# Local attention and a squared-ReLU MLP in one kernel: how the probabilities of the last three blocks are transposed

## The chip, the cores and the metric

The kernel runs on one core of a Trainium2 chip. The metric is the device time of one execution in microseconds (us). The times of the kernel before are 823.29, 822.72 and 823.01 us, median 823.01. A core has a matrix engine (TensorE, "PE" in the profile, with its weight loads as "PEld"), VectorE (DVE), ScalarE (ACT), GpSimd (POOL) and SyncE (SP), which here only issues DMA transfers. SBUF is the on-chip memory of 128 partitions, PSUM the accumulation memory that TensorE writes.

## The reference

```python
def _attn_ref(q, k, v):                       # 8 batches, 8 heads, 576 tokens, 64 wide; chunks of 64 tokens
    scores = scale * np.matmul(q_c, k_c.transpose(0, 1, 2, 4, 3))
    scores = scores - np.max(scores, axis=-1, keepdims=True)
    attn = np.exp(scores)
    attn = attn / (np.sum(attn, axis=-1, keepdims=True) + 1e-09)
    out = np.matmul(attn, v_c)
...
def _moe_ref(x, w_in, w_out, s, b):           # 4608 tokens, 512 -> 2048 -> 512
    h = x @ w_in
    r = np.maximum(h, 0.0)
    g = s * (r * r) + b
    return (g @ w_out).astype(np.float32)
```

All in float32. The output of the attention, tokens by 512, is the input x of the MLP.

## The kernel before

The 4608 tokens are 36 tiles of 128. A first stage computes four of them and prepares the weights; then come four blocks of eight tiles (`Block`; block 1 is the subclass `Second`). Each block is a list of steps. A step is twelve matmuls of 128x128 by 128x512 on TensorE, three for each float32 product, since every operand is held as a high and a low part ("gh" and "gl" for the down layer, "xh" and "xl" for the up layer). Blocks 2, 3 and 4 have 28 up steps and 28 down steps, seven products of half-size blocks in place of eight, whose sums VectorE forms (class `Chain`); block 1 has 32 up steps in the ordinary way, beside which it combines the weights of the later blocks (`combine`), and 28 down steps. Work that goes beside the matmuls is hung on the step before which it is written: `pre[step]` is a list of calls that every engine gets in this order. So the program fixes the order on every engine; an engine runs ahead or behind as its semaphores allow.

Beside its own matmuls each block computes the attention of the next block's tokens, in four groups of two tiles. In blocks 2 and 3 the groups begin at steps 3, 14, 25 and 36, in block 1 at 5, 17, 30 and 42 (`GROUPS`); below, a group is called by its first step, so "group 25 of block 2". Counted from its first step n, a group does (`plan_attention`): loads of q, k and v at n-3; at n the scores, 32 matmuls of 64x64 into PSUM (S, line 207); at n+1 the row maxima and the subtraction on VectorE (lines 212, 216); at n+2 the exponential on ScalarE; at n+3 the row sums, at n+4 the division ("norm", lines 228 to 230), all on VectorE; at n+7 eight transposes of 128x128 on TensorE into PSUM (T, line 237); at n+8 two copies of these to SBUF on ScalarE (line 242); at n+9 the product with v, 32 matmuls of 64x64 (V, line 249); at n+10 two copies of the result on ScalarE (line 273). S, T and V all take their PSUM tile from the pool `ps_a`, which has one buffer: whichever comes next waits until the engine that reads the one before has done so.

The other PSUM tiles come from `ps`, three buffers. Nearly all SBUF tiles come from one pool of 45 buffers (`slots`). The weights of each step are streamed from DRAM by SP, 512 KB a step, requested six steps ahead into six buffers (line 372), so SP keeps pace with TensorE; SP works in order, and an instruction that waits holds all behind it. GpSimd does the remaining sums, 128x1024 in float32, in the down steps of blocks 2 to 4 (line 413), and the differences of x (line 353); in block 1 those of line 413 are on VectorE.

Of the kernel before, what the change touches and what calls it, by code (L numbers as in the profile page):

```python
# [27 lines left out]
def local_attention_then_squared_relu_mlp(ctx: ExitStack, tc, qkv, w, s, b, out):  # L28
    nc = tc.nc
    P = 128  # L30
    NTB, NPAIR = qkv.shape[0], w.shape[1]
    NJ = 2 * NPAIR
    DM = out.shape[0]
    HALF = DM // 2
    CH = D = 64
    H = DM // D
    NHP = H // 2
    LAG = 3
    N = 2
    G = N * NHP  # L40
    NPP = NPAIR // 2
    BLOCK = 8
    assert NTB % BLOCK == 4

    const = ctx.enter_context(tc.tile_pool(name="const", bufs=1))
# [10 lines left out]
    def slot(dtype=F32, name="s"):  # L56
        return slots.tile([P, 2, DM], dtype, name=name, tag="s")
# [29 lines left out]
    class Pair:  # L87


        def __init__(self, k):  # L90
            self.layer, self.k = sequence[k]
            self.words = self.f = None
# [86 lines left out]
    class Attention:  # L179
        def __init__(self, tb, bank, x=None, col=0):  # L180
            self.tb, self.bank = tb, bank
            self.x = x and [t[:, :, col:col + N * P].rearrange("p a (i t) -> p i a t", i=N) for t in x]

        def load_qk(self):
            t = [slot(name="qk") for _ in range(N)]
            for i in range(N):
                nc.sync.dma_start(out=t[i], in_=qkv[self.tb + i, :, 0:2, :])
            self.qk = [t.rearrange("p i (h t) -> p i h t", h=H) for t in t]

        def load_v(self):  # L190
            t = slot(name="v")
            for i in range(N):
                nc.sync.dma_start(out=t[:, i], in_=qkv[self.tb + i, :, 2, :])
            self.v = [t[:, i].rearrange("p (h d) -> p h d", h=H) for i in range(N)]
# [8 lines left out]
        def scores(self):  # L203
            self.ps = self.bank(0)[:, :, 0:G * CH].rearrange("p c (g k) -> p c g k", g=G)
            for i, hp, c, h, rows, cols in self.quarters():
                qk = self.qk[i]
                nc.tensor.matmul(out=self.ps[cols, c, i * NHP + hp, :], lhsT=qk[rows, 0, h, :], rhs=qk[rows, 1, h, :],  # L207
                                 start=True, stop=True)

# [29 lines left out]
        def copies(self):  # L239
# [2 lines left out]
                nc.scalar.copy(out=pT[:, i, :], in_=self.ps[:, i, :])  # L242
            self.pT = pT.rearrange("p i (a t) -> p i a t", a=NHP)

        def values(self, apart=False):
            tiles = [self.bank(2) for _ in range(N if apart else 1)]
            ps = [t[:, :, 0:G * CH].rearrange("p c (g t) -> p c g t", g=G) for t in tiles]
            for i, hp, c, h, rows, cols in self.quarters():
                nc.tensor.matmul(out=ps[i if apart else 0][cols, c, i * NHP + hp, :], lhsT=self.v[i][rows, h, :],  # L249
                                 rhs=self.pT[rows, i, hp, cols], start=True, stop=True)  # L250
            if apart:
                self.halves = [(ps[i][:, :, i * NHP:(i + 1) * NHP, :].rearrange("p c a t -> p a c t"),
                                *(x[:, i].rearrange("p a (c t) -> p a c t", c=2) for x in self.x)) for i in range(N)]
            elif self.x:
                self.halves = [(ps[0][:, c].rearrange("p (i a) t -> p i a t", i=N),
                                *(x[:, :, :, c * CH:(c + 1) * CH] for x in self.x)) for c in range(2)]
            else:
                self.xf = slot(name="xf").rearrange("p i (a t) -> p (i a) t", a=2)
                x = self.xf.rearrange("p a (i t) -> p i a t", i=N)
                self.halves = [(ps[0][:, c].rearrange("p (i a) t -> p i a t", i=N), x[:, :, :, c * CH:(c + 1) * CH])  # L260
                               for c in range(2)]
# [68 lines left out]
    class Block:  # L330
        UP, TILES, ORDER, GROUPS = 28, 56, (0, 2, 1, 3), (3, 14, 25, 36)

        def __init__(self, n):
            self.tb0 = 4 + (n - 1) * BLOCK
            self.groups = [Attention(self.tb0 + 2 * i, steady_bank) for i in self.ORDER]
# [150 lines left out]
            at(24, lambda: self.store(0, 1, self.down_chain.c12))  # L486
            at(28, lambda: self.store(1, 0, self.down_chain.c21))

        def plan_attention(self, n, a):
            self.at(max(n - 3, 0), a.load_qk, a.load_v)  # L490
            for k, *fs in ((0, a.scores), (1, a.peak, a.sub), (2, a.exp), (3, a.sum), (4, a.norm),
                           (7, a.transposes), (8, a.copies), (9, a.values), (10, a.x_out)):
                self.pre[n + k][:0] = fs

        def plan_following(self, following):
            for n, a in zip(self.GROUPS, following.groups):
                self.plan_attention(n, a)
            z = self.GROUPS[-1] + 5
            self.at(z, lambda: following.x_sums(0))
            for k, i in enumerate(ORDER):  # L500
                self.at(z + 2 + k, lambda i=i: following.x_split(0, i))
                self.at(min(z + 8 + k, self.slots - 1), lambda i=i: following.x_split(1, i))
            self.pre[z + 6].insert(0, lambda: following.x_sums(1))
# [146 lines left out]
    one, two = (Attention(i, first_bank, x, i * P) for i in (0, N))  # L650
    blocks = [(Second if n == 1 else Block)(n) for n in range(1, (NTB - 4) // BLOCK + 1)]
    for block, following in zip(blocks, blocks[1:] + [None]):
# [180 lines left out]
```

## Time and profile before

| | before |
|---|---|
| times of three runs | 823.29, 822.72, 823.01 us |
| time of the profiled execution | 822.79 us |
| its span, first to last instruction | 821.0 us |
| TensorE busy | 789.7 us, 96% of the span |
| VectorE busy | 612.8 us, 75% |
| ScalarE busy | 451.2 us, 55% |
| GpSimd busy | 157.5 us, 19% |
| mean granted TensorE clock | 0.992 |

The profiled execution is one execution, and its span is 1.8 us shorter than its time. A row of the timeline gives the start, the duration, the engine, the line, the operation, the tiles written and read, and in square brackets how long the engine had been idle before and what ended that. Matmuls are pipelined, so their durations overlap; the cost of a group of them is read from the starts of the large matmuls around it.

### The profile page before, as it was taken

What the parts mean: (1) busy time and instruction counts of PE and PEld (TensorE: products, weight loads), DVE (VectorE), ACT (ScalarE), POOL (GpSimd) and SP (SyncE); (2) the same over time, 40 slices, a digit from 0 to 9 for tenths busy, and PEclk for the clock granted to TensorE, in tenths of its full rate; (3) what the DMA queues carried; (4) which work ended last, traced back from release to release, by engine and by line L of the source; (5) the groups of instructions that cost most, each with busy time, mean ns of one, the idle gap of its engine ahead of it and who ended that gap; (6) DMA issues with size and microseconds to landing.
All of it is one profiled execution on the core that took longest, in us unless ns stands there. A gap on an engine that the chain in (4) does not pass through costs nothing.

```text
span 821.0 us, 13827 instructions
## 1 busy us (share of the span) xinstructions
PE 789.7 (96%) x5658; PEld 649.7 (79%) x5658; DVE 612.8 (75%) x602; ACT 451.2 (55%) x530; POOL 157.5 (19%) x73
## 2 busy tenths in 40 slices
PE   8779889999999999999999999999999999999996
PEld 7658777787887888888888888888888888888885
DVE  6899995478868887668599875775998846669651
ACT  5767763565655465465575553556736535565621
POOL 2333330000000211000347210002381201027000
PEclk9999999999999999999999999999999999999999
DMA  8899977298799556765664658746556575556552
GB/s 337 285 399 329 327 266 288 104 337 292 250 306 319 214 205 235 292 246 182 240 224 180 224 199 337 252 173 246 192 188 241 186 277 197 189 197 193 219 194 87
DMA packets 82210, 198.03 MB, mean 241 GB/s; under 512 B 6372, under 2 KB 37092, under 8 KB 82148
## 3 DMA queue, kind: packets, MB, share of 16 engines
q1 hardware_dynamic: 82144, 197.16, 68.2%
q8 instruction: 45, 0.74, 0.4%
q14 instruction: 17, 0.14, 0.1%
q10 hardware_dynamic: 4, 0.00, 0.0%
HBM read 156.24 MB, written 40.89 MB: 240 GB/s over the span
## 4 chain that ended last, share of the span: by engine, by line
PE 76%; DVE 10%; DMA 6%; ACT 4%; issue 3%; POOL 1%; SPq 1%; ACTq 0%; DVEq 0%; POOLq 0%
PE ps L426 35%; PE ps L396 28%; PE ps L556 5%; DMA raw<-in_w_dram 4%; PE ps_a L249 2%; PE ps_o L636 2%; PE ps_a L207 1%; PE ps_a L237 1%; DVE f L160 1%; POOL f L126 1%; DVE f L120 1%; DVE wl L134 1%; DVE p L230 1%; DVE wl L170 1%; DMA v<-in_qkv_dram 1%
## 5 line engine op out<-in xcount | busy, mean ns | idle before, releaser
L426 PE MATMUL ps<-gh,st 128*128 128x512 f32 x896 | 280.6, 391 | 0.0
L396 PE MATMUL ps<-xh,st 128*128 128x512 f32 x672 | 211.1, 391 | 0.0
L287 DVE TENSOR_TENSOR gl<-q,gh 128x1024 fp32r<-128x1024 f32 x112 | 176.3, 1597 | 34.8 <-ACT gh L286 34.3
L426 PEld LDWEIGHTS ps<-gh,st 128*128 128x128 f32 x896 | 168.2, 188 | 35.3
L426 PE MATMUL ps<-gl,st 128*128 128x512 f32 x448 | 174.4, 389 | 0.0
L396 PEld LDWEIGHTS ps<-xh,st 128*128 128x128 f32 x672 | 126.1, 188 | 26.5
L413 POOL TENSOR_TENSOR q<-q 128x1024 f32<-128x1024 f32 x24 | 72.7, 3047 | 306.2 <-PE ps L396 223.8
L396 PE MATMUL ps<-xl,st 128*128 128x512 f32 x336 | 130.8, 389 | 0.0
L286 ACT CAST gh<-q 128x1024 fp32r<-128x1024 f32 x112 | 113.1, 1049 | 9.0 <-DVE q L413 8.5
L426 PEld LDWEIGHTS ps<-gl,st 128*128 128x128 f32 x448 | 84.1, 188 | 16.9
L301 DVE TENSOR_TENSOR q<-ps,tmp 128x1024 f32<-128x1024 f32 x48 | 58.7, 1222 | 47.3 <-PE ps L396 44.5
L401 ACT ACTIVATE q<-q 128x1024 f32<-128x1024 f32 x48 | 51.0, 1063 | 72.0 <-DVE q L301 71.8
L301 DVE TENSOR_TENSOR tmp<-ps,tmp 128x1024 f32<-128x1024 f32 x48 | 58.5, 1219 | 37.8 <-PE ps L396 32.1
L586 ACT ACTIVATE o<-o,bias,sb 128x512 f32<-128x512 f32 x32 | 24.4, 809 | 109.9 <-DVE o L301 109.9
L556 PE MATMUL ps<-xh,st 128*128 128x512 f32 x256 | 81.6, 393 | 1.1 <-issue 1.1
L396 PEld LDWEIGHTS ps<-xl,st 128*128 128x128 f32 x336 | 63.1, 188 | 12.8
L353 POOL TENSOR_TENSOR xt<-xf 128x512 f32<-128x512 f32 x12 | 19.2, 1602 | 219.4 <-DVE gl L287 162.5
L556 PEld LDWEIGHTS ps<-xh,st 128*128 128x128 f32 x256 | 48.1, 188 | 11.7 <-issue 1.5
L126 POOL TENSOR_TENSOR f<-f,raw 128x1024 int32<-128x1024 int32 (+1 forms) x17 | 39.4, 2320 | 75.5 <-DVE f L120 46.5
L402 ACT ACTIVATE q<-q 128x1024 f32<-128x1024 f32 x48 | 50.9, 1061 | 1.5
L556 PE MATMUL ps<-xl,st 128*128 128x512 f32 x128 | 49.9, 390 | 0.0
L413 DVE TENSOR_TENSOR q<-q 128x1024 f32<-128x1024 f32 x40 | 48.6, 1220 | 0.5
(79 smaller groups left out, 941.3 us busy)
## 6 DMA issues: line engine op xcount, KB each, us to landing
st<-kept SPq DMA_DIRECT2D x212, 512.0 KB, 4.3
qk<-in_qkv_dram SPq DMA_DIRECT2D x36, 512.0 KB, 6.3
raw<-in_w_dram SPq DMA_DIRECT2D x32, 512.0 KB, 7.3
kept<-wh SPq DMA_DIRECT2D x24, 512.0 KB, 6.5
kept<-wl SPq DMA_DIRECT2D x24, 512.0 KB, 7.3
v<-in_qkv_dram SPq DMA_DIRECT2D x36, 256.0 KB, 6.8
out_dram<-o SPq DMA_DIRECT2D x18, 512.0 KB, 3.1
kept<-wh SPq DMA_DIRECT2D x8, 384.0 KB, 7.8
```

The source lines that it names most:

```text
L126: nc.gpsimd.tensor_tensor(out=i, in0=i, in1=low.bitcast(I32), op=ALU.add)
L286: nc.scalar.copy(out=hi[:, :, cols], in_=parts)
L287: nc.vector.tensor_tensor(out=lo[:, :, cols], in0=parts, in1=hi[:, :, cols].bitcast(F32), op=ALU.subtract)
L301: nc.vector.tensor_tensor(out=to, in0=self.ps[product], in1=x, op=ALU.add)
L353: engine.tensor_tensor(out=to, in0=x, in1=y, op=ALU.subtract)
L396: nc.tensor.matmul(out=to[:, k], lhsT=a[:, cols], rhs=x[:, c, :], start=c == 0 and n == 0, stop=c == 1 and n == 2)
L401: nc.scalar.activation(out=q, in_=q, func=AF.Relu)
L402: nc.scalar.activation(out=q, in_=q, func=AF.Square)
L413: engine.tensor_tensor(out=self.q[to, pp], in0=self.q[x, pp], in1=self.q[y, pp], op=ALU.subtract)
L426: nc.tensor.matmul(out=self.to[:, d], lhsT=a[:, cols], rhs=x[:, k, :], start=pp == 0 and k == 0 and n == 0, stop=pp == NPP - 1 and k == 1 ...
L556: nc.tensor.matmul(out=self.bank[:, k], lhsT=a, rhs=x[:, c, :], start=d == 0 and c == 0 and n == 0, stop=d == 1 and c == 1 and n == 2)
L586: nc.scalar.activation(out=to[:, d], in_=source[:, d], func=AF.Identity, scale=s_col, bias=bias[:, d0 + d:d0 + d + 1])
```

## The change

For the groups of blocks 2, 3 and 4 (tiles 12 to 35, `turned`; their attention is computed during blocks 1, 2 and 3, twelve groups in all), the transposes on TensorE and the copies on ScalarE are left out. Instead VectorE transposes the 128x1024 tile of probabilities in blocks of 32x32 (`turn`, at n+5), and eight transfers within SBUF, each of 32 partitions by 512 elements (64 KB), put the blocks in place (`swap`, at n+6, on SP). The scores are laid out with the chunk in the partitions and the head in the columns, for which the host lays out q and k of these tiles by head. V reads its probabilities as two runs of 32 columns. V and the copies behind it move to the third and fourth step of the group that follows (`following + 3`, `following + 4`), for the last group of a block to n+9 and n+10 as before; the loads move from n-3 to n-5.

```diff
+    TURNED = 4 + BLOCK
...
+            self.turned = tb >= TURNED
...
+            if self.turned:
+                self.qk = [t.rearrange("p i (a c) t -> p i a c t", a=NHP) for t in self.qk]
...
+                if self.turned:
+                    nc.tensor.matmul(out=self.ps[rows, h % 2, i * NHP + hp, :], lhsT=qk[cols, 0, hp, c, :],
+                                     rhs=qk[cols, 1, hp, c, :], start=True, stop=True)
+                    continue
...
+        def turn(self):
+
+            self.t = slot(name="pB")
+            nc.vector.transpose(out=self.t.rearrange("p b (n k) -> p b n k", k=32),
+                                in_=self.p3.rearrange("p n (b k) -> p b n k", b=2))
+
+        def swap(self):
+
+            pT = slot(name="pT")
+            for c in range(2):
+                for k in range(2):
+                    for q in range(2):
+                        nc.sync.dma_start(out=pT[64 * c + 32 * k:64 * c + 32 * k + 32, q], in_=self.t[64 * c + 32 * q:64 * c + 32 * q + 32, k])
+            self.pT = pT.rearrange("p q (g h t) -> p g h q t", g=G, h=2)
+
...
-                                 rhs=self.pT[rows, i, hp, cols], start=True, stop=True)
+                                 rhs=self.pT[rows, i * NHP + hp, h % 2] if self.turned else self.pT[rows, i, hp, cols],
+                                 start=True, stop=True)
...
-        def plan_attention(self, n, a):
-            self.at(max(n - 3, 0), a.load_qk, a.load_v)
-            for k, *fs in ((0, a.scores), (1, a.peak, a.sub), (2, a.exp), (3, a.sum), (4, a.norm),
-                           (7, a.transposes), (8, a.copies), (9, a.values), (10, a.x_out)):
-                self.pre[n + k][:0] = fs
+        def plan_attention(self, a, n, following):
+            self.at(max(n - 5, 0), a.load_qk, a.load_v)
+            for k, *fs in ((n, a.scores), (n + 1, a.peak, a.sub), (n + 2, a.exp), (n + 3, a.sum), (n + 4, a.norm),
+                           (n + 5, a.turn), (n + 6, a.swap), (following + 3, a.values), (following + 4, a.x_out)):
+                self.pre[k][:0] = fs
...
-            for n, a in zip(self.GROUPS, following.groups):
-                self.plan_attention(n, a)
+            for a, *places in zip(following.groups, self.GROUPS, self.GROUPS[1:] + (self.GROUPS[-1] + 6,)):
+                self.plan_attention(a, *places)
```

The order on VectorE in blocks 2 and 3, around the division of group 25 and the subtraction of group 36 (p<-p,z is the division, p<-ps_a,m the subtraction, gl the low parts for the down steps, o the first output of the block). Before:

```order
L230 TENSOR_TENSOR p<-p,z 128x1024
L413 TENSOR_TENSOR q<-q 128x1024 x2
L287 TENSOR_TENSOR gl<-q,gh 128x1024 x6
L301 TENSOR_TENSOR o<-ps,tmp 128x1024
L212 TENSOR_REDUCE m<-ps_a 128x16
L216 TENSOR_TENSOR p<-ps_a,m 128x2x8x64
```

Now (line numbers of the changed kernel):

```order
L238 TENSOR_TENSOR p<-p,z 128x1024
L256 STREAM_TRANSPOSE pB<-p 128x1024
L437 TENSOR_TENSOR q<-q 128x1024 x2
L311 TENSOR_TENSOR gl<-q,gh 128x1024 x6
L325 TENSOR_TENSOR o<-ps,tmp 128x1024
L220 TENSOR_REDUCE m<-ps_a 128x16
L224 TENSOR_TENSOR p<-ps_a,m 128x2x8x64
```

The transpose of group 25 stands ahead of the nine instructions that lead to the subtraction of group 36, and V of group 25, which before stood two steps ahead of the scores of group 36, now needs the PSUM buffer that this subtraction reads.

The order of SP's transfers around the loads of q, k and v for group 36 in block 2 (st is a step's weights, pT<-pB the eight transfers). Before:

```order
L372 DMA st<-kept_3_83 128x1024 x6
L187 DMA qk<-in_qkv_dram 128x1024 x2
L193 DMA v<-in_qkv_dram 128x512 x2
L372 DMA st<-kept_3_83 128x1024
L372 DMA st<-kept_0_84 128x1024
```

Now:

```order
L396 DMA st<-kept_3_83 128x1024 x4
L265 DMA pT<-pB 32x512 x8
L189 DMA qk<-in_qkv_dram 128x1024 x2
L197 DMA v<-in_qkv_dram 128x512 x2
L396 DMA st<-kept_3_83 128x1024 x3
L396 DMA st<-kept_0_84 128x1024
```

The eight transfers of group 25 stand directly ahead of the four loads, and the loads two steps earlier in the stream of weights.

## Rows read from the trace of the kernel before

**Rows 1.** The first part of the page: busy time of each engine, its share of the span, instructions.

```profile
PE 789.7 (96%) x5658; PEld 649.7 (79%) x5658; DVE 612.8 (75%) x602; ACT 451.2 (55%) x530; POOL 157.5 (19%) x73
```

**Rows 2.** The waits of TensorE from 200 us to the end: who waited for whom, us in total, times, longest.

```profile
PE ps_a L249 <- ACT pT L242: 1.2, 1, 1.2
```

**Rows 3.** Groups of instructions by line from 176 us to the end, which holds the twelve groups: T on TensorE and the copies of its result on ScalarE (busy us, mean ns of one, idle before).

```profile
L242 ACT COPY pT<-ps_a 128x512 f32<-128x512 f32 x24 | 12.9, 590 | 14.9 <-PE ps_a L237 14.6
...
L237 PE MATMUL ps_a<-ident,p 128*128 128x128 f32 x96 | 12.4, 272 | 0.2 <-DVE p L230 0.2
```

**Rows 4.** The timeline of TensorE around T of group 25 in block 2, and around V of that group.

```profile
424.15 0.39 PE L426 MATMUL ps<-gl,st 128*128 128x512 f32 x1
424.38 0.39 PE L426 MATMUL ps<-gh,st 128*128 128x512 f32 x1
424.61 1.03 PE L237 MATMUL ps_a<-ident,p 128*128 128x128 f32 x8
425.40 0.48 PE L426 MATMUL ps<-gh,st 128*128 128x512 f32 x1
425.71 0.40 PE L426 MATMUL ps<-gl,st 128*128 128x512 f32 x1
...
430.71 0.39 PE L426 MATMUL ps<-gh,st 128*128 128x512 f32 x1
431.03 1.16 PE L249 MATMUL ps_a<-pT,v 64*64 64x64 f32 x64
432.12 0.50 PE L426 MATMUL ps<-gh,st 128*128 128x512 f32 x1
432.46 0.39 PE L426 MATMUL ps<-gl,st 128*128 128x512 f32 x1
```

**Rows 5.** The timeline of TensorE in block 1 where it waits: V of group 5, T and V of group 30.

```profile
189.58 1.16 PE L249 MATMUL ps_a<-pT,v 64*64 64x64 f32 x64 [1.84 <-ACT pT L242]
...
259.53 1.06 PE L237 MATMUL ps_a<-ident,p 128*128 128x128 f32 x8 [0.20 <-DVE p L230]
...
267.29 1.16 PE L249 MATMUL ps_a<-pT,v 64*64 64x64 f32 x64 [1.23 <-ACT pT L242]
```

**Rows 6.** The timeline of VectorE in block 2, from its last wait for TensorE (near step 25) to the last instruction ahead of the place where the transpose of group 36 is put; several equal instructions without a gap are one row (xN).

```profile
404.44 1.23 DVE L301 TENSOR_TENSOR tmp<-ps,tmp 128x1024 f32<-128x1024 f32 x1 [1.50 <-PE ps L396]
...
420.46 1.22 DVE L230 TENSOR_TENSOR p<-p,z 128x1024 f32<-128x1024 f32 x1
421.60 2.48 DVE L413 TENSOR_TENSOR q<-q 128x1024 f32<-128x1024 f32 x2
424.00 18.98 DVE L287 TENSOR_TENSOR gl<-q,gh 128x1024 fp32r<-128x1024 f32 x6
442.90 1.21 DVE L301 TENSOR_TENSOR o<-ps,tmp 128x1024 f32<-128x1024 f32 x1
445.27 1.23 DVE L216 TENSOR_TENSOR p<-ps_a,m 128x1024 f32<-128x1024 f32 x1
...
454.73 1.22 DVE L301 TENSOR_TENSOR tmp<-ps,tmp 128x1024 f32<-128x1024 f32 x1
```

**Rows 7.** The timeline of TensorE in block 2: S of group 36 with the first matmul of step 36, and V of group 36.

```profile
437.79 1.16 PE L207 MATMUL ps_a<-qk 64*64 64x64 f32 x64
438.88 0.50 PE L426 MATMUL ps<-gh,st 128*128 128x512 f32 x1
...
464.48 1.16 PE L249 MATMUL ps_a<-pT,v 64*64 64x64 f32 x64
```

**Rows 8.** Block 1: ScalarE's last wait for TensorE before the down steps; then VectorE's timeline around the division of group 30, the first output and the subtraction and division of group 42; then TensorE: S of group 42 with the first matmul of step 42, and V of group 42.

```profile
232.62 1.02 ACT L561 ACTIVATE q<-ps 128x1024 f32<-128x1024 f32 x1 [0.74 <-PE ps L556]
...
255.27 1.23 DVE L287 TENSOR_TENSOR gl<-q,gh 128x1024 fp32r<-128x1024 f32 x1 [1.54 <-ACT gh L286]
...
276.46 1.22 DVE L301 TENSOR_TENSOR o<-ps,tmp 128x1024 f32<-128x1024 f32 x1
...
285.96 1.22 DVE L216 TENSOR_TENSOR p<-ps_a,m 128x1024 f32<-128x1024 f32 x1
...
294.36 1.22 DVE L230 TENSOR_TENSOR p<-p,z 128x1024 f32<-128x1024 f32 x1
...
276.77 1.16 PE L207 MATMUL ps_a<-qk 64*64 64x64 f32 x64
277.87 0.50 PE L426 MATMUL ps<-gh,st 128*128 128x512 f32 x1
...
303.47 1.16 PE L249 MATMUL ps_a<-pT,v 64*64 64x64 f32 x64
```

**Rows 9.** The timeline of SP around the loads of group 36 in block 2, then, from the lists by line, the time from issue to landing of the stores of 512 KB (line 589) and of the loads of v, 256 KB (line 193).

```profile
425.17 0.90 SPq L187 DMA_DIRECT2D qk<-in_qkv_dram  x2
426.17 0.93 SPq L193 DMA_DIRECT2D v<-in_qkv_dram  x2
...
DMA to landing us min/median/max: 2.8/3.1/4.8
...
DMA to landing us min/median/max: 5.4/6.8/9.4
```

**Rows 10.** The timeline of GpSimd in block 2 beside the six gl of rows 6.

```profile
423.05 16.61 POOL L413 TENSOR_TENSOR q<-q 128x1024 f32<-128x1024 f32 x5 [12.12 <-DVE q L413]
```

More of the change, by code (lines that the diff above doesn't have):

```diff
@@ L813, in tokens, with by_chunk, by_head @@
         return a.transpose(0, 2, 1, 3).reshape(NTOK // P, 2, P // 2, H, D)
-    qT, kT = (tokens(a).transpose(0, 1, 4, 3, 2).reshape(NTOK // P, P, DM) for a in (q, k))
+    def by_chunk(a):
+        return a.transpose(0, 1, 4, 3, 2).reshape(-1, P, DM)
+    def by_head(a):
+        a = a.transpose(0, 3, 4, 1, 2)
+        return a.reshape(-1, H // 2, 2, D, 2, P // 2).transpose(0, 2, 3, 1, 4, 5).reshape(-1, P, DM)
+    qT, kT = (np.concatenate([by_chunk(tokens(a)[:12]), by_head(tokens(a)[12:])]) for a in (q, k))
     qkv = np.stack([qT, kT, tokens(v).reshape(NTOK // P, P, DM)], axis=2)
```

## The prediction

> **What bounds the kernel now.** I read the busy times first. TensorE is busy 96% of the span, VectorE 75%, ScalarE 55% [rows 1]; the granted clock is 0.99. Then TensorE's waits: from 200 us to the end, while the blocks run, it waits for other engines 1.2 us at the longest kind [rows 2]. So in this part almost every microsecond taken from TensorE would shorten the span, as long as the others keep up. That makes the timeline of VectorE the second view: has it room, and which of its instructions does TensorE need soon after they end? In blocks 2 and 3 VectorE waits for TensorE at 404.44 and then works without a gap past the subtraction of group 36, which ends at 445.27 + 1.23 = 446.50 [rows 6]. In block 1 the last wait of the elementwise engines for TensorE before the down steps is one of 0.74 us on ScalarE at 232.62; VectorE runs from 255.27 on and ends the subtraction of group 42 at 285.96 + 1.22 = 287.18 [rows 8]. In these stretches VectorE does not follow TensorE; it is the slower one, and only lead time hides it.
>
> **What the change removes.** T: eight transposes put 425.40 behind 424.38, where the next matmul would follow 0.23 later, and the one after it comes 0.08 late as well (425.40 to 425.71 against 0.23): 1.02 - 0.23 + 0.08 = 0.88 us [rows 4]. Twelve groups (96 transposes, [rows 3]): 10.6 us on TensorE. The 24 copies of 590 ns on ScalarE [rows 3], 14 us, are off the path except where V waited for them: 1.84 and 1.23 us in block 1, and T waited 0.20 there for the division [rows 5], together 3.3 us. If nothing took their place the change would give 10.6 + 3.3 = 13.9 us.
>
> **What it adds on VectorE.** One transpose of 128x1024 in float32 for each group. The trace shows none. From below: a VectorE instruction of that size that follows another costs 421.60 - 420.46 = 1.14 us, 1.22 by itself [rows 6]. From above: 18.98 / 6 = 3.16 us, what the six gl take beside GpSimd's additions [rows 6, 10]. I take 1.2, because the new instruction stands ahead of the sums that release GpSimd. The Trainium skill ("VectorE: DVE Perf Modes", The three transpose paths) gives VectorE 311 ns for one 128x128 tile in bfloat16, and its Rules for kernel authors send a 128x128 transpose to TensorE; eight such tiles would be an estimated 2.5 us, and the sum below would be 4 us higher by it. No run here shows one yet.
>
> **What it moves: V.** Before, V of a group stood well ahead of the scores of the next; now it stands three steps behind them, and S and V share one PSUM buffer. So V must wait until VectorE has subtracted the next group's maxima. This is the term that decides, and I work it out block by block. A step is 12 x 0.227 = 2.7 us. V itself costs 432.12 - 430.71 - 0.23 + 0.11 = 1.29 us [rows 4].
>
> Blocks 2 and 3, V of group 25, now at step 39. Step 36 began at 438.88, so step 39 at 447.0 [rows 7]. By then three T are gone (2.64) and V of group 25 is no longer behind (1.29): TensorE gets there at 443.1. The subtraction of group 36 ended at 446.50. VectorE's run starts from TensorE's step 25, which comes earlier by two T and by V of group 14, moved from step 23 to 28: 3.05; and it holds the transpose of group 25: +1.2. So 444.65. TensorE waits 1.5 us. Four T saved less this wait: 3.5 - 1.5, with rounding 2.1 us gained in each of the two blocks.
>
> Block 1, V of group 30, now at step 45. Step 42 began at 277.87, step 45 thus at 286.0 [rows 8]. TensorE would get there earlier by three T (2.64), the waits (3.3) and the V moved behind it (1.29): 278.8. The subtraction of group 42 ended at 287.18; work passes between ScalarE and VectorE from 232.62 on, and the wait there allows at most 0.74 less; the transpose of group 30 adds 1.2 (that of group 5 and of group 17 fall into VectorE's idle time, of which it has 208 us in all [rows 1]): 287.6. TensorE waits 8.8 us. V follows, and step 45 begins 1.1 later at 288.7, that is 2.7 later than before; the fourth T gives 0.9 back. Block 1 loses 1.8 us, all its savings gone into this one wait.
>
> **What it adds on SP.** Eight transfers for each group. Issues in a row take (426.17 + 0.93 - 425.17) / 4 = 0.5 us each [rows 9], so the eighth is issued 3.4 us after the first. Landing is not shown for 64 KB; from above 6.8 (v, 256 KB), from below under 2.8 (512 KB to DRAM, the quickest) [rows 9]. I take 3.0, near the stores, since little is in the queue then: 6.4 us from the end of the transpose. Nothing needs them soon except the last group of a block. There: in block 2 the instruction ahead of the transpose ended at 455.95 [rows 6], now 455.95 - 3.05 + 1.2 = 454.1, the transpose at 455.3; V stood at 464.48 [rows 7], now 464.48 - 3.5 + 1.5 = 462.5: 7.2 us. In block 1 division at 295.58, one gl and the transpose, with the shift of 0.5: 298.4; V at 303.47 + 2.7 - 0.9 = 305.3: 6.9 us. Both just hold. Behind the waiting transfers stand the loads and the stream of weights, which is five steps, 13.6 us, ahead; the worst place is group 30 of block 1, where SP waits some 10 us for VectorE, and a stall of TensorE from it falls ahead of the 8.8 us wait and inside it.
>
> The layouts of S and V (rows and columns of the array exchanged, two runs of 32 columns) I cost at nothing: S and V take 1.16 us alike, though their layouts differ already [rows 4, 7]. From above they could take twice that, 1.16 x 24 = 28 us if nothing hid it; a gain is excluded to below the 0.018 us at which their 64 instructions now follow each other.
>
> **The sum.** +1.8 - 2.1 - 2.1 = -2.4 us on the profiled execution, whose span is 821.0 and whose time 822.8: 820.4. The median of the three runs is 0.2 above that execution: **820.6 us**. Own range: the transpose at 1.0 to 1.6 us enters three times (-0.6 to +1.2), block 1's start 0 to 1.5: 818.5 to 823.5.
>
> **Rivals.**
> 1. *TensorE's saving arrives.* For it: 96% busy and no waits [rows 1, 2]. Against: the two waits above, each from rows. If block 1's engines do follow TensorE (ScalarE is freed of eight copies there), its 6.8 us arrive in part or whole: 823.0 - 6.8 - 4.2 = 812; with no wait in blocks 2 and 3 either, 809.
> 2. *The transfers decide (the other side).* Place: V of the last group in each block. They decide once transpose to landing takes over 7 us. Landing as v does, 6.8, makes 3.4 + 6.8 = 10.2, so 3.2 us late, three times: 820.6 + 9.6 = 830. For it: one queue, in order, with 512 KB a step in it. The Trainium skill ("DMA: Bandwidth & Descriptors", Rules for kernel authors) says that small transfers are mostly overhead, and that transfers to separate partitions share the same engines and should be one; with its fixed 2 us and 436 GB/s a piece would take an estimated 2.15 us, and eight end to end 17. Against that last reading: four loads in 1.9 us land after 5.4 to 9.4 each [rows 9], so they overlap.
> 3. *The transpose is dear*: 2.5 to 3.2 us, 1.3 to 2.0 more, three times: 824.5 to 826.5. For it only GpSimd's presence [rows 10].
> 4. *The change does not save T's time*, because the new layouts of S and V slow them by half: 12 groups x 1.2, in part inside the waits: about 832.
>
> **Chances.** Forecast 0.42, rival 1 0.20, rival 2 0.23, rival 3 0.10, rival 4 0.05. Under 0.2%, 1.65 us, a measurement of this kernel cannot tell a difference from none. The forecast's own range lies 0.55 faster, 0.4 same; with rival 1 faster 0.43; same 0.17 plus small forms of rivals 2 and 3, 0.25; slower 0.32. Eight in ten: 811 to 830.
>
> **What would show it.** No T after 176 us, 0.88 us less at each place. TensorE's waits: V on VectorE's subtraction, one of 6 to 9 us in block 1 near step 45, one of 1 to 2 in each of blocks 2 and 3; a wait of V on the transfers only if rival 2 holds. The VectorE transpose at 1.1 to 1.3 us. VectorE's run in block 2 one instruction longer. The forecast is wrong if V waits nowhere, or if a wait appears on the weights.

## The result, and the profile after

The changed kernel takes 829.71 us (median of four runs, 828.26 to 829.86), the kernel before 822.87 beside it: ratio 1.0086, 95% interval 1.0074 to 1.0097. It is slower by about 6.9 us, where I forecast 820.6 us, 2.4 less than before on the profiled execution. The profiled execution of the changed kernel has a span of 827.9 us, the one before 821.0.

First where the 6.9 us lie. This table takes, from the timelines of TensorE, the start of each block's first 128x512 matmul, and gives the differences between them:

| from block to block, us | block 1 | block 2 | block 3 | block 4 to the end |
|---|---|---|---|---|
| before | 183.3 | 166.5 | 166.5 | 158.9 |
| after | 189.1 | 167.2 | 167.2 | 158.9 |

Block 1 loses 5.8, blocks 2 and 3 lose 0.7 each. (Its start moves by some 2 us between the profiled executions, 144.1 to 146.3, since the first stage varies; so I compare lengths of blocks.) Block 4, beside which no attention is computed, is the same.

The first part of the page of the changed kernel, to set beside [rows 1]:

```profile
PE 786.4 (95%) x5562; PEld 645.2 (78%) x5562; DVE 630.4 (76%) x614; ACT 438.9 (53%) x506; POOL 156.5 (19%) x73
```

TensorE has 96 instructions less, the transposes. Its waits from 150 us to the end, which answer to [rows 2, 5]:

```profile
PE ps L450 <- DMA st<-kept: 5.5, 2, 4.9
PE ps_a L272 <- issue: 4.6, 2, 2.6
PE ps_a L212 <- DVE bias L813: 3.5, 1, 3.5
```

So three kinds of wait are new, 13.6 us, and the ones before, of 1.84 and 1.23 us on ScalarE, are gone. TensorE's timeline at the four longest of them, and at one V that did not wait (291.28) (start, duration, in brackets the wait), with one or two matmuls behind; L272 is V, L212 the scores, L450 the down matmuls:

```profile
237.14 1.58 PE L212 MATMUL ps_a<-qk 64*64 64x64 f32 x64 [3.50 <-DVE bias L813]
...
276.24 0.77 PE L450 MATMUL ps<-gh,st 128*128 128x512 f32 x1 [4.90 <-DMA st<-kept]
276.80 0.63 PE L450 MATMUL ps<-gl,st 128*128 128x512 f32 x1
...
291.28 1.16 PE L272 MATMUL ps_a<-pT,v 64*64 64x64 f32 x64
...
451.41 1.16 PE L272 MATMUL ps_a<-pT,v 64*64 64x64 f32 x64 [1.97 <-issue]
452.50 0.63 PE L450 MATMUL ps<-gh,st 128*128 128x512 f32 x1
452.94 0.63 PE L450 MATMUL ps<-gl,st 128*128 128x512 f32 x1
...
456.72 0.62 PE L450 MATMUL ps<-gh,st 128*128 128x512 f32 x2
457.18 0.39 PE L450 MATMUL ps<-gl,st 128*128 128x512 f32 x1
...
618.61 1.16 PE L272 MATMUL ps_a<-pT,v 64*64 64x64 f32 x64 [2.65 <-issue]
```

"issue" means that the view names no engine. VectorE's timeline does. The first row is the transpose of group 30 in block 1, the others are of block 2:

```profile
262.85 1.24 DVE L256 STREAM_TRANSPOSE pB<-p 128x1024 f32<-128x1024 f32 x1
...
425.29 1.25 DVE L256 STREAM_TRANSPOSE pB<-p 128x1024 f32<-128x1024 f32 x1
...
428.82 18.97 DVE L311 TENSOR_TENSOR gl<-q,gh 128x1024 fp32r<-128x1024 f32 x6
...
450.09 1.23 DVE L224 TENSOR_TENSOR p<-ps_a,m 128x1024 f32<-128x1024 f32 x1
```

The subtraction of group 36 ends at 450.09 + 1.23 = 451.32, and V of group 25 starts at 451.41: it is the wait for the shared PSUM buffer.

The rows behind V show something else. Matmuls of 0.63 us stand 0.44 apart (452.50 to 452.94), where those behind 456.72 stand 0.23 apart. The windows of that stretch give the reason. A row has the stretch, its length, the busy time (and instructions) of PE, PEld, DVE, ACT and POOL, then the clock granted to TensorE, the share of the DMA engines and their GB/s. The last row is of block 1, behind the wait for weights:

```profile
448.00:450.00 2.00, 1.45 (x7) 0.87 (x5) 2.00 (x2) 1.04 (x2) 2.00 (x2) 1.00 0.00 0
450.00:452.00 2.00, 0.59 (x38) 0.62 (x42) 1.83 (x3) 2.00 (x3) 1.41 (x2) 1.00 0.30 115
452.00:454.00 2.00, 2.00 (x44) 1.64 (x36) 1.30 (x2) 2.00 (x3) 0.00 (x0) 0.68 1.03 311
454.00:456.00 2.00, 2.00 (x6) 1.52 (x6) 2.00 (x3) 2.00 (x4) 0.00 (x0) 0.50 0.98 328
456.00:458.00 2.00, 2.00 (x10) 1.67 (x9) 1.93 (x4) 2.00 (x4) 0.00 (x0) 0.97 0.97 393
...
278.00:280.00 2.00, 2.00 (x6) 1.53 (x5) 0.00 (x0) 2.00 (x3) 0.00 (x0) 0.50 1.04 406
```

Behind the wait the granted clock falls to 0.50, the lower of its two levels (1.2 of 2.4 GHz). Step 39 takes 456.95 - 452.50 = 4.45 us instead of 2.7. So a wait of 2.0 us costs 3.7. The Trainium skill ("TensorE: Matmul & The Clock Gate", HAM oscillation — how this bites in real kernels) says that work behind a wait for a transfer starts at the lower clock; the trace agrees at 276.24 and shows the same behind waits for VectorE, though not behind every one (e10 below).

In block 1, SP's timeline shows why the weights came late (L265 the transfers, L396 the weights, L175 stores of combined weights):

```profile
252.33 3.05 SPq L396 DMA_DIRECT2D st<-kept  x2
264.12 4.95 SPq L265 DMA_DIRECT2D pT<-pB  x8
269.16 0.53 SPq L175 DMA_DIRECT2D kept<-wh  x1
269.73 0.53 SPq L175 DMA_DIRECT2D kept<-wl  x1
270.36 0.98 SPq L396 DMA_DIRECT2D st<-kept  x1
```

SP stands from 255.38 to 264.12 at the first transfer of group 30, until the transpose has ended (262.85 + 1.24 = 264.09), then issues eight transfers at 0.62 us each and two stores. The weights of step 41 are asked for at 270.36, land 5.74 us later, and TensorE starts at 276.24.

The offset of a step's first 128x512 matmul, after less before, adds it up (TensorE's timelines; V's own 1.2 us, which moved behind, is counted out of the wait column, and in block 1 the slow scores and the slow matmul right behind the waits of 3.50 and 4.90 us are counted in it):

| place | offset at the step, then at the next | wait that is new | half clock behind |
|---|---|---|---|
| block 1, steps 29 to 31 | -5.3, -1.3, -0.2 | 4.0 | 1.1 |
| block 1, steps 40 to 42 | -2.8, +2.3, +5.0 | 5.1 | 2.7 |
| block 2, steps 38 to 40 | +2.1, +5.3, +7.1 | 2.0 | 1.8 |
| block 3, steps 38 to 40 | +2.2, +6.1, +7.8 | 2.7 | 1.7 |

13.8 us of waits and 7.3 us of half clock have eaten more than the 13.9 us that the removed parts gave. A wait of 0.62 us for weights at 441.02, in block 2, is not in the table.

### The profile page after: what moved, and what is told of

It reads as the page before. It is cut to its first block, busy times and chain, and to the rows that moved or that the text cites. A ratio compares the mean times of both kernels' runs of the same rounds, so it can differ in the third digit from the quotient of the medians.

```text
span 827.9 us, 13819 instructions
## 1 busy us (share of the span) xinstructions
PE 786.4 (95%) x5562; PEld 645.2 (78%) x5562; DVE 630.4 (76%) x614; ACT 438.9 (53%) x506; POOL 156.5 (19%) x73
## 4 chain that ended last, share of the span: by engine, by line
PE 72%; DVE 12%; DMA 7%; issue 3%; ACT 3%; SPq 1%; POOL 1%; ACTq 0%; DVEq 0%; POOLq 0%
PE ps L450 35%; PE ps L420 27%; PE ps L580 5%; DMA raw<-in_w_dram 3%; PE ps_a L272 2%; PE ps_o L660 2%; DMA st<-kept 2%; DVE gl L311 1%; DVE f L161 1%; PE ps_a L212 1%; DVE wl L135 1%; DVE f L121 1%; DMA kept<-wl 1%; DMA kept<-wh 1%; DVE m L220 1%
## 5 line engine op out<-in xcount | busy, mean ns | idle before, releaser
L450 PE MATMUL ps<-gh,st 128*128 128x512 f32 x896 | 283.9, 396 | 5.5 <-DMA st<-kept 5.5
L311 DVE TENSOR_TENSOR gl<-q,gh 128x1024 fp32r<-128x1024 f32 x112 | 179.7, 1626 | 33.8 <-ACT gh L310 33.5
L450 PEld LDWEIGHTS ps<-gh,st 128*128 128x128 f32 x896 | 171.0, 191 | 42.5 <-issue 6.0
L450 PE MATMUL ps<-gl,st 128*128 128x512 f32 x448 | 176.8, 395 | 0.0
L450 PEld LDWEIGHTS ps<-gl,st 128*128 128x128 f32 x448 | 85.3, 190 | 17.4
L377 POOL TENSOR_TENSOR xt<-xf 128x512 f32<-128x512 f32 x12 | 19.3, 1608 | 228.8 <-PE ps L450 167.0
```

What stands on the lines that cost most here:

```text
L311: nc.vector.tensor_tensor(out=lo[:, :, cols], in0=parts, in1=hi[:, :, cols].bitcast(F32), op=ALU.subtract)
L377: engine.tensor_tensor(out=to, in0=x, in1=y, op=ALU.subtract)
L450: nc.tensor.matmul(out=self.to[:, d], lhsT=a[:, cols], rhs=x[:, k, :], start=pp == 0 and k == 0 and n == 0, stop=pp == NPP - 1 and k == 1 ...
```

## The experiments

Theories. A: the loss is TensorE's waits (V behind the subtraction, weights behind the transfers, scores behind the bias) and the half clock behind each. A': in block 1 these waits stand in for each other. B: the new operations cost it by themselves. D, formed on the way: VectorE and ScalarE bound these stretches, so every wait removed comes back. The diffs below give the changed places in short form, not the whole edit.

**V in the step ahead of the next scores** (e1), instead of three behind; the last group of a block as it was:

```diff
-  (following + 3, a.values), (following + 4, a.x_out)
+  (following - 1, a.values, a.x_out)
```

> Theory A (waits): in blocks 2 and 3 V of the third group, three steps behind the scores of the fourth, waits 2.0 and 2.7 us for VectorE's subtraction because both use the one PSUM buffer, and the clock granted behind each wait falls to half, which costs another 1.8 and 1.7 us. With V in the step ahead of the next group's scores these waits go and nothing replaces them: 829.7 - 2.0 - 1.8 - 2.7 - 1.7 = 821.5 us; block 1 keeps its waits (3.5 us for the bias, 4.9 us for weights). Theory B (the new operations themselves, transpose, transfers and layouts, cost the time wherever V stands): 828.5 to 831. Theory C (V ahead of the scores finds the transfers not landed): a wait of V on the transfers, 823 or more.

Measured 827.29 us (ratio 1.0055, 1.0040 to 1.0070); blocks 190.6, 165.4, 165.0. In blocks 2 and 3 the waits for the subtraction went and no step ran at the lower clock, but the gain was 1.8 and 2.2 us, not 3.8 and 4.4. Block 1 grew, since there V now met the bias:

```profile
PE ps L450 <- DMA st<-kept: 5.2, 2, 5.0
PE ps_a L272 <- DVE bias L819: 4.4, 1, 4.4
PE ps_a L272 <- DMA pT<-pB: 2.4, 2, 1.3
```

So B falls for blocks 2 and 3 (the operations are all there, and the blocks are shorter than in the kernel before), C holds in part (the last V of a block waited 1.1 and 1.3 us for its transfers), and A was too optimistic about what stands behind a wait.

**The transfers on GpSimd's queue** (e2):

```diff
-  nc.sync.dma_start(out=pT[64 * c + 32 * k:64 * c + 32 * k + 32, q], in_=self.t[64 * c + 32 * q:64 * c + 32 * q + 32, k])
+  nc.gpsimd.dma_start(out=pT[64 * c + 32 * k:64 * c + 32 * k + 32, q], in_=self.t[64 * c + 32 * q:64 * c + 32 * q + 32, k])
```

> The eight transfers of a group are issued by GpSimd, which is idle in block 1, not by SP; V stands as in the changed kernel. Theory A: the wait of TensorE for weights near step 40 of block 1 (4.9 us, and 2.7 us of half clock behind it) comes from SP standing at the transfers until the transpose has ended; it goes. V of group 30 would then be reached 7.8 us earlier, at 283.5, and the subtraction of group 42 ends about 283.6, so little is waited there: 829.7 - 7.8 = 821.9 us, waits of blocks 2 and 3 unchanged. Theory A' (the prediction's: one wait in block 1 takes the place of the other): V of group 30 waits 4 to 8 us, 826 to 830. Theory B: 828.5 to 831.

Measured 837.40 us (1.0166 to 1.0204); blocks 187.1, 174.9, 170.4. Block 1 behaved as A' says: no wait for weights, and V of group 30 waited 3.9 us for the subtraction in its place; 2.0 us gained of 7.8. Blocks 2 and 3 lost 7.7 and 3.2, for a reason I had not put a number on: GpSimd's sums were held behind its own transfers and then came in one run, and a gl of VectorE that began beside them did not end before they did. GpSimd, then VectorE, block 2; the last row is the list by line for that gl alone (duration in ns, three times the same, then its start):

```profile
423.68 3.42 POOL L265 DMA_DIRECT2D pT<-pB  x7 [0.36 <-issue]
427.12 16.44 POOL L437 TENSOR_TENSOR q<-q 128x1024 f32<-128x1024 f32 x7
```

```profile
430.63 20.80 DVE L311 TENSOR_TENSOR gl<-q,gh 128x1024 fp32r<-128x1024 f32 x4 [3.73 <-ACT gh L310]
...
L311 DVE TENSOR_TENSOR gl<-q,gh x1: 15231/15231/15231, 430.6 to 430.6; 128x1024 fp32r<-128x1024 f32 x1
```

The first of these four gl took 15.23 us, from 430.63 to 445.86, past the end of the seven sums at 443.56; the other three shared the remaining 5.6 us. In [rows 6] a gl took 3.16 us on average. TensorE waited 5.45 us for the long one, and in blocks 2 and 3 another 5.8 us at V for the transfers, three waits of up to 2.0 us.

**V six steps behind the next scores** (e4), transfers and the last group unchanged:

```diff
-  (following + 3, a.values), (following + 4, a.x_out)
+  (following + 6, a.values), (following + 7, a.x_out)
```

> V of the first three groups six steps behind the scores of the next, not three; transfers on SP as in the changed kernel. Theory A: the waits for the subtraction in blocks 2 and 3 and the half clock behind them go, block 1 stays: 821.5 us. Theory B: 828.5 to 831.

Measured 825.03 us (ten runs, 823.51 to 828.27; 1.0025 to 1.0051); the profiled execution, 827.7, is at the upper end: blocks 188.3, 166.0, 166.9. No V waits for a subtraction now, and half of the expected gain arrives. What took its place, in the same view as above:

```profile
PE ps L450 <- DMA st<-kept: 9.5, 4, 5.2
```

Four waits for weights, of which 5.2 us in block 1 and the others in blocks 2 and 3, where the transfers stand ahead of loads and weights too.

**Both, e4 and e2 together** (e5):

> Both: V six steps behind the next scores and the transfers issued by GpSimd. Theory A: the two gains add, 829.7 - 8.2 - 7.8 = 813.7 us, with only the wait for the bias in block 1 left. If GpSimd's issues hold up its own sums in blocks 2 and 3, 816 to 822. Theory B: 828.5 to 831.

Measured 834.48 us (1.0130 to 1.0164); blocks 186.8, 173.6, 169.6. GpSimd's queue spoils it as in e2: V waited 9.1 us for the transfers, and TensorE 3.5 us for a gl.

**Only V moved, in the kernel before** (b1); TensorE's transposes and ScalarE's copies stay:

```diff
-  (9, a.values), (10, a.x_out)
+  (following - n + 3, a.values), (following - n + 4, a.x_out)
```

> The kernel before with nothing changed but the place of V (three steps behind the scores of the next group); TensorE still transposes, ScalarE copies. Theory A: in block 1 the two waits for the copies (3.1 us) go, but V of group 30 is reached at 286.2 - 3.1 - 1.3 = 281.8 and waits for the subtraction of group 42, which ends at 287.2: 5.4 us and some 2 us of half clock, together 2.3 + 2 = +4; in blocks 2 and 3 nothing is saved, V is reached at 445.9 when the subtraction has ended (445.2): 0. So 824 to 828 us. Theory B (the new operations cost the time, the place of V nothing): 819.5 to 823.

Measured 825.57 us (ten runs, 823.43 to 827.66; 1.0025 to 1.0051); blocks 184.9, 166.5, 166.5. The move alone costs 1.6 us in block 1 of the profiled execution (3 us by the medians) and nothing in blocks 2 and 3. Its waits:

```profile
PE ps_a L249 <- DVE p L216: 3.4, 1, 3.4
PE ps_a L207 <- DVE bias L789: 1.7, 1, 1.7
```

This is the wait that I put at 8.8 us in the changed kernel, at the place where I put it, with no lower clock behind it in this execution.

**Block 1's groups as before, only those of blocks 3 and 4 turned** (e10); the groups that are not turned have the loads and steps of the kernel before:

```diff
-    TURNED = 4 + BLOCK
+    TURNED = 4 + 2 * BLOCK
```

> The change for the groups of blocks 3 and 4 alone (eight groups, computed during blocks 2 and 3); the four groups computed during block 1 as before. Theory A: block 1's loss of 5.4 us goes, blocks 2 and 3 lose 0.8 and 0.7 us as in the changed kernel: 822.7 + 1.5 = 824.2 us. If each new operation cost the same wherever it stands, eight of twelve groups would keep 4.6 of the 6.9 us: 827.3.

Measured 823.31 us (1.0004 to 1.0025); blocks 183.3, 168.4, 165.6. A holds: block 1's loss is gone. The two last lengths are worth a look: blocks 2 and 3 do the same work, V waits the same 2.65 us in both, and yet one is 1.9 longer than before and the other 0.9 shorter. TensorE at V in block 2 and in block 3, then the windows there:

```profile
444.84 1.99 PE L272 MATMUL ps_a<-pT,v 64*64 64x64 f32 x64 [2.65 <-issue]
...
613.28 1.16 PE L272 MATMUL ps_a<-pT,v 64*64 64x64 f32 x64 [2.65 <-issue]
```

```profile
446.00:448.00 2.00, 2.00 (x35) 1.69 (x28) 1.30 (x3) 2.00 (x3) 0.00 (x0) 0.50 1.05 279
448.00:450.00 2.00, 2.00 (x6) 1.52 (x6) 2.00 (x3) 2.00 (x4) 0.00 (x0) 0.50 0.98 391
...
614.00:616.00 2.00, 2.00 (x38) 1.65 (x30) 1.30 (x2) 2.00 (x3) 0.00 (x0) 1.00 1.02 297
```

The clock fell behind the one, where V itself took 1.99 us, and stayed behind the other. So the fall is a price of its own, beside the wait, here 2.8 us by the lengths of the two blocks, and the same wait does not always pay it.

**The wait filled with matmuls** (e15), ahead of V at the end of step 38 of blocks 2 and 3:

```diff
+  if self.UP == 28 and (i, pp) == (2, 2) and self.following:
+      for d in range(2):
+          ...
+          for a, x in ((h, gh), (h, gl), (l, gh), (h, gh)):
+              nc.tensor.matmul(out=self.to[:, d], lhsT=a[:, cols], rhs=x[:, 1, :], start=False, stop=False)
```

> The changed kernel, with eight more matmuls of 128x512 (1.8 us) on TensorE ahead of the wait of V in blocks 2 and 3; they add products to a PSUM sum a second time, so the outputs of these blocks differ from the reference. Theory A: TensorE is busy in most of the 2.0 and 2.7 us that it waited, the granted clock does not fall behind it, and steps 39 and 40 lose their 1.8 and 1.7 us: 826.2 us, less than the changed kernel in spite of more work. If the slow steps behind the wait have another cause (weights, transfers): 829.5 to 830.5.

Measured 826.83 us (1.0034 to 1.0060), with more work 2.9 us less than the changed kernel; blocks 188.6, 165.6, 165.6. In block 2, L457 are the added matmuls; the last row is the window behind V:

```profile
449.25 0.61 PE L457 MATMUL ps<-gh,st 128*128 128x512 f32 x2
449.80 1.16 PE L272 MATMUL ps_a<-pT,v 64*64 64x64 f32 x64
450.89 0.50 PE L450 MATMUL ps<-gh,st 128*128 128x512 f32 x1
451.23 0.39 PE L450 MATMUL ps<-gl,st 128*128 128x512 f32 x1
451.46 0.62 PE L450 MATMUL ps<-gh,st 128*128 128x512 f32 x2
...
450.00:452.00 2.00, 2.00 (x69) 1.75 (x63) 1.30 (x2) 2.00 (x3) 0.00 (x0) 1.00 0.96 295
```

V starts with TensorE busy up to it, the matmuls behind stand 0.34 and then 0.23 apart, as behind V in [rows 4], and the granted clock stays at 1.00. In blocks 2 and 3 the half clock is thus shown to hang on TensorE's standing idle, and not on weights or transfers. That it does so in block 1 too is read from its rows and was not tried.

**Transfers two steps later, V three behind** (e13, first + line), and **both later** (e6, second). The last group is as it was in e13, and in e6 has its transfers at n+6 as before and V and its copies at n+10:

```diff
-  (n + 6, a.swap), (following + 3, a.values), (following + 4, a.x_out)
+  (n + 8, a.swap), (following + 3, a.values), (following + 4, a.x_out)
+  (n + 8, a.swap), (following + 6, a.values), (following + 7, a.x_out)
```

> Only the transfers moved two steps later (the last group's stay); V as in the changed kernel, three steps behind the next scores. Theory A' (one wait takes the other's place): the wait for weights in block 1 goes, and V of group 30 then waits 3.5 to 4.5 us for the subtraction of group 42, with some 1 us of half clock, as the run with GpSimd's transfers showed; blocks 2 and 3 keep their waits: 827 to 828.5 us. If the wait for weights was a cause by itself: 829.7 - 7.8 = 822.

> As e4 (V six steps behind the next scores), and the transfers, on SP, two steps later, so that SP reaches them when the transpose has ended and the weights go ahead of them; the last group's V one step later. Theory A: the wait for weights in block 1 goes and V stands behind the subtraction: block 1 -2.5 us (as the run with both changes and GpSimd showed up to step 49), blocks 2 and 3 -3 and -2.6 us: 814.6 us. Rival D (VectorE's and ScalarE's chain bounds these stretches, and each wait removed comes back at the next thing that needs it): 819 to 823.

e13: 826.22 us (1.0023 to 1.0067); blocks 186.9, 166.8, 167.0. As A' says: no wait for weights, and V of group 30 waits 3.87 us for the subtraction in its place. e6: 815.83 us (0.9904 to 0.9934); blocks 182.0, 163.6, 164.0. It beats both kernels, and D, which said 819 to 823, does not hold for the kernel as a whole. All of TensorE's waits in it:

```profile
PE ps_a L212 <- DVE bias L818: 2.5, 1, 2.5
PE ps L450 <- DMA st<-kept: 2.3, 3, 1.4
```

| us | transfers at n+6 | transfers at n+8 |
|---|---|---|
| V three behind the next scores | 829.7 | 826.2 |
| V six behind | 825.0 | 815.8 |

The edits gain 4.7 and 3.5 alone and 13.9 together: each alone leaves or uncovers the wait that the other removes (5.2 us for weights in e4, 3.87 us of V in e13). (In e6 the last group's V also stands one step later, which was not tried apart.)

**V ahead of the next scores, transfers later** (e7, e1's places with e6's for the transfers):

> As e1 (V in the step ahead of the next scores), with the transfers two steps later as in e6. Theory A: no wait for weights; V of group 17 in block 1 still meets the bias computation in the PSUM buffer (4.4 us): block 1 about +1, blocks 2 and 3 about -1.8 each: 820 us. Rival D: 823 to 827.

Measured 828.71 us (1.0056 to 1.0101); blocks 190.0, 167.2, 166.5. A miss: later transfers landed late for an early V (seven waits, 3.8 us), the scores waited up to 3.6 us for ScalarE's copies of V's result, and V of group 17 still waited 4.4 us for the bias.

**The bias later, on top of e6** (e14), `b1.at(33, biases)` for `b1.at(28, biases)`:

> The kernel of e6 with the bias computation, which takes the one PSUM buffer ahead of the scores of group 30 in block 1, five steps later (33, not 28). Theory A: the wait of these scores for it (2.5 us) and the half clock behind it (0.6 to 0.9) go: 815.8 - 3.2 = 812.6 us. Rival D (VectorE's and ScalarE's chain bounds block 1 there, the wait comes back at the next thing): 815 to 816.5.

Measured 816.12 us (0.9899 to 0.9945), as e6; blocks 181.7, 163.8, 165.0. The wait came back at once, 3.4 us of the bias matmuls for the subtraction of group 30. At this place D is right: the wait removed came back.

**What e6 owes to the place of V alone**: the kernel before with V later. b2 put V six steps behind, b3 three in block 1 (five for its third group) and six elsewhere.

> The kernel before, TensorE's transposes and ScalarE's copies kept, with V six steps behind the next scores as in e6. What e6 owes to the new transposes: theory A: the waits for the copies in block 1 (3.1 us) go, blocks 2 and 3 stay: 819.6 us; e6 at 815.8 has 3.8 us more from the transposes taken off TensorE. If the place of V explained all of e6: 816. If nothing: 822.7.

> The kernel before with V later, without the collision of b2: in block 1 V three steps behind the next scores for the first two groups, five for the third; in blocks 2 and 3 six. TensorE's transposes stay. Theory A: blocks 2 and 3 stay as they are; in block 1 the waits for the copies go (3.1 us) and 1.7 us come back at the bias: 821.3 us, so that most of what e6 gains (815.8) is owed to the transposes taken off TensorE. If the place of V explained e6: 816.

b2 took 832.49 us (1.0092 to 1.0150), blocks 194.0, 166.5, 166.5: in block 1 T came one step behind V and waited 3.3 and 5.3 us for ScalarE to clear the PSUM buffer, a collision that this kernel brought in, so it does not price V's place in block 1. b3: 821.02 us beside 821.27, ratio 1.0000 (0.9990 to 1.0011); blocks 182.6, 166.5, 166.5. With TensorE's transposes in place, V's place gains nothing in blocks 2 and 3.

**e6 with block 1's groups as before** (e12):

> e6 with the four groups computed during block 1 left as in the kernel before. Theory A: block 1 0, blocks 2 and 3 -2.9 and -2.4 us as in e6: 822.7 - 5.3 = 817.4 us, so block 1's groups give e6 only the 1.3 us between. If the change pays in block 1 as in the others (3 us): 818.8.

Measured 817.50 us beside 821.27 (0.9934 to 0.9969); blocks 183.3, 163.7, 164.3. The time is the expected one, but the kernel before was quicker beside it than the 822.7 from which the expectation was worked out: 3.8 us are saved, not 5.3. By the lengths of the blocks most of e6's gain is the transposes taken off TensorE in blocks 2 and 3: 2.7 and 2.1 us here, 2.8 and 2.5 in e6, of the 3.5 that four T cost. Block 1 adds 1.4 in e6 by its length. By the medians (6.8 us saved by e6, 3.8 by e12) it could be up to 3; the intervals do not separate the two.

## Why the prediction was wrong

The removed part was right: T's 0.88 us show at each place in blocks 2 and 3 (the offset falls by 0.79 at the step and another 0.1 at the next), and the copies' waits went.

The transpose, by the list of groups by line (busy, mean ns):

```profile
L256 DVE STREAM_TRANSPOSE pB<-p 128x1024 f32<-128x1024 f32 x12 | 14.9, 1239 | 0.1
```

1.24 us, forecast 1.2. Rival 3, and the estimate of 2.5 us from the Trainium skill ("VectorE: DVE Perf Modes", The three transpose paths), fall. The scores and V take 1.16 us as before at full clock: rival 4 falls.

The transfers: the list of DMA issues on the page (KB each, median us from issue to landing) has

```profile
pT<-pB SPq DMA_DIRECT2D x96, 64.0 KB, 2.0
```

so they land after 2.0 us, below the 2.8 of the stores, where I took 3.0; issues take 0.62 us, not 0.5. From the transpose's end to the last landing 270.54 - 264.09 = 6.45 us in block 1, forecast 6.4. V of the last group did not wait in the changed kernel: rival 2 falls at the place that I gave. The estimate of 17 us end to end, worked out from the fit in the Trainium skill ("DMA: Bandwidth & Descriptors", Anatomy of one DMA — SWDGE (gpsimd) path), whose figures are for transfers issued by GpSimd, falls too: one piece lands after about the 2 us of the fit, but the eight overlap.

V in blocks 2 and 3: forecast to wait 1.5 us, measured 1.97 and 2.65. Right in place and cause, short in length. (In the sum, 3.5 - 1.5 is 2.0 and not 2.1; nothing hangs on it.)

Block 1: I had one wait of 8.8 us at V of group 30. It came as 3.5 us at the scores of group 30 (the bias, in the same PSUM buffer, is late on VectorE) and 4.9 us for weights; V then waited for nothing (291.28 above). Together 8.4, and that this is near 8.8 is luck: neither part was in the sum, and a wait on the weights was my own sign that the forecast is wrong. I wrote that the stall behind SP falls ahead of V's wait and inside it. VectorE's timeline shows that it does not fit inside:

```profile
284.87 1.23 DVE L224 TENSOR_TENSOR p<-ps_a,m 128x1024 f32<-128x1024 f32 x1
```

The subtraction of group 42 ended at 286.10, and TensorE came to V 5.2 us later. In e2 and e13, without the stall, V waits 3.9 us each, and block 1 is still 2.0 and 2.2 us shorter than in the changed kernel. So the stall, which I had put at nothing, is a second step that failed, worth some 2 us with the clock behind it. The bias as a user of `ps_a` I had overlooked.

**The step that failed** is the one under all of these: "TensorE waits 1.5 us", "8.8 us", and a sum made of the waits' lengths alone. I priced a wait at its length. The half clock behind the waits, 7.3 us, is missing from the sum. My forecast of the span was 821.0 - 2.4 = 818.6, the measured one 827.9: of the 9.3 us between, 7.3 are half clock, 1.6 the longer waits in blocks 2 and 3 (4.6 for 3.0) and 0.6 the wait for weights in block 2, against which block 1 began 0.3 earlier. With these 7.3 us the forecast's -2.4 becomes +4.9. In blocks 2 and 3 the two misses belong together: behind waits of 1.5 us, as forecast, no profile here shows a lower clock, behind the 1.97 and 2.65 us that came it fell. That the half clock costs these times is shown by e15 for blocks 2 and 3 (3.1 us of the 3.5); the 3.8 us of block 1 are read from its rows.

The kernel before did give a warning, outside the rows that I had picked. In the blocks its longest wait, 1.84 us at 189.58, is followed by full clock. But in the first stage TensorE waits 3.98 us, and behind that the matmuls stand 0.43 apart at half clock:

```profile
36.37 0.68 PE L609 MATMUL ps_h<-xh,wh 128*128 128x512 f32 x1 [3.98 <-DVE r L617]
36.85 0.63 PE L609 MATMUL ps_h<-xl,wh 128*128 128x512 f32 x1
37.27 0.63 PE L609 MATMUL ps_h<-xh,wl 128*128 128x512 f32 x1
...
38.00:40.00 2.00, 2.00 (x6) 1.52 (x6) 1.97 (x4) 1.66 (x3) 0.00 (x0) 0.51 0.99 383
...
190.00:192.00 2.00, 2.00 (x58) 1.71 (x50) 1.97 (x2) 1.51 (x2) 0.00 (x0) 1.00 0.87 268
```

So a wait of some 9 us, as I forecast for block 1, could have been priced from the trace of before. The mean granted clock of 0.99, which I read, hides such stretches.

Rival 1, the saving that arrives, is what e6 shows in part, 6.8 of the 13.9 us, once V and the transfers have other places.

## What to carry over

A saving on the busiest engine turns into a wait at the next thing that it reaches too early, so ask of each shared buffer and each in-order queue how much lead is left, and move the consumers with the saving. Two waits in a row hide each other: undoing one shows little, so test the fixes together as well as alone. And look through the whole trace of before, its first stage too, for what follows a long wait of TensorE: here the waits of 1.97 to 4.90 us in the changed kernel cost up to 1.9 times their length, because of the clock behind them.

## What the runs showed that was not expected

Over all profiles here, no wait of TensorE up to 1.84 us inside the blocks was followed by a lower clock where no longer wait stood next to it. Behind those of 1.86 to 5.45 us the lost time was between nothing (2.00 us in e2, 2.65 in block 3 of e10, 3.41 in b1) and 2.8 us (2.65 in block 2 of e10); behind the waits for weights of 4.88 to 5.21 us in block 1 it was about 2.5, counted from the pitch of the 128x512 matmuls. It does not simply grow with the wait; what else decides was not tried.

VectorE's gl depend on what GpSimd does beside them: 1.22 us in block 1 of the changed kernel, where GpSimd adds nothing (261.71), 3.40 to 3.42 beside GpSimd's sums in block 2 of the kernel before, and one of 15.23 in e2, where seven of these sums ran without a gap. What decides when such a gl can end is not shown here.
